# Where the projection slices are computed, and the order of the table rounds, in a two-part kernel on Trainium2

## The chip, the cores and the metric

The kernel runs on one core of one Trainium2 chip. The metric is the device time of one execution in microseconds. A core has five engines with queues of their own, each in order: PE (matrix products), DVE (VectorE), ACT (ScalarE), POOL (GpSimd) and SP (SyncE, which here only starts transfers). They wait for each other by semaphores.

## The reference

Two independent computations share the input and are joined along the last axis:

- Part A, a recurrent memory attention. The sequence of 2048 rows is cut into 64 segments of 32. Each segment attends over 8 memory rows and its own 32, with 32 heads of 128; the first 8 rows of its output are the memory of the next segment. So the segments are sequential.
- Part B, a state space convolution. `K = einsum(C, exp(dt*A*l), dt*B).real` for 2048 positions and 1024 channels, then `irfft(rfft(u)*rfft(K))`, plus `u*Dskip`.

```python
h = jnp.concatenate([mem, xs], axis=1)
q, k, v = (jnp.einsum('btd,dhe->bhte', h, W) for W in (Wq, Wk, Wv))
...
K = jnp.einsum('dn,dnl,dn->dl', Cc, P, dB).real
y = irfft2(rfft2(u) * rfft2(K))[..., :L] + u * Dskip
```

## The kernel before

The order of work is written out by hand: each engine executes its instructions in the order in which the program issues them. In time there are four stretches:

1. **The parameter stage** (0 to about 91 us). DVE and ACT compute, from A, B, C and dt, the log modulus and the angle of each coefficient in float32 (`modulus`, `angle`); `put3` splits each in three bfloat16 parts and stores them to the DRAM tensors PB (cast to `hi` and `mid` on ACT, differences on DVE, stores on SP). Beside that, the generator `matrices` makes the Fourier matrices MF with sines on ACT, two columns a step. The generator `ahead.transposes` (lines 84 to 104) loads x in 16 blocks on POOL's queue, transposes them on PE, and copies each on ACT into `xst`, stored to XTd, and into `xTl`, the 8 last rows of each segment. `run` takes one step of each of its generators in turn.
2. **The table rounds** (91 to about 460 us), the loop `for f in range(-1, 17)`. 16 rounds go over the blocks of 64 channels. Each round takes the words of ORDER one by one. A word is an operation and a slot; with a prime it belongs to the round before. X..t and X..p are the matmuls of the phases (`ptt`, two PSUM buffers) and of the powers (`pa`, one buffer); E is exp, k the shift by a magic constant (both ACT), n the turns (DVE), S the sine (ACT), b the absolute value (DVE), C the cosine (ACT), w the negation `wn` (DVE), gi and gr the products with the exps (DVE, `products`, two instructions each of bfloat16 operands), K the matmuls of kernel values and x their copy to `KxT`. Exp and sine need different tables, so ACT loads a table twice a round. The projections of part A (generator `pro`), the Fourier transform of u (`bg`) and the transposes of MF (`mb`) go along as side work: P, U and M issue their matmuls into a PSUM tile of the pool of four, and p, A, u and m evict it. ON_ACT and ON_DVE say which engine evicts which slot.
   - One slice of `pro` is 8 matmuls of 512 columns (k and q, line 158) or 16 of 256 (v, line 145), and one cast out of PSUM. Two slices use one 512 KB load of weights (`wsl`, four buffers, SP's queue). There are 96 slices; k and q of them need the whole of `xTl`.
   - `bg` (function `side`) yields four pieces per block of u: a copy (r=0), adds on DVE (r=2), a copy (r=1), adds on DVE (r=3). After the last, POOL adds and subtracts the float32 results (`ux`, lines 882 to 885) and stores them to Ud from its own queue. Behind that in POOL's queue stand the four loads of the next round's parameters (`load_par`, issued in E0). The first round already runs U2 and U3, so the pieces fall to the slots in the order 2, 3, 0, 1.
3. **Spectra and inverse transform** (460 to about 720 us). It starts in round 16, at the first word of ORDER, with `negate` on DVE and `spectrum(0)` on PE, beside the rest of the last table.
4. **The 64 segments of part A** (to the end), which read what the projections stored (PKd, XTd).

Four slices of `pro` are issued between the parameter stage and the loop, evicted in turn by ACT and DVE (lines 1110 to 1115); the rounds take six each. The transposes are spread over the two calls of `run` at the end of the parameter stage.

Of the kernel before, what the change touches and what calls it, by code (L numbers as in the profile page):

```python
# [16 lines left out]
PSUM = bass.MemoryType.PSUM  # L17
# [568 lines left out]
def bcast_front(ap, n):  # L586
# [10 lines left out]
NF = NP + NN  # L597
NE, NT = NC + NF, NC + NA
PLEN = 4096
ORDER = ("X0p' X0t' P3' b0' w0' C0' b1' P4' p3' C1' gi0' U2' P5' gr0' k0 n0 P0 E0 gr1' p4' X1t X1p p5' k1 X2t P1 E1 n1 p0 A1' k2 w1' X2p n2 "  # L600
         "X3t E2 U3' gi1' p1 X3p k3 X4t P2 E3 n3 k4 u1' X4p X5t p2 E4 U0 n4 k5 X5p n5 K0' E5 A0 X6p X6t E6 M' X7t k6 m' X7p U1 E7 x0' k7 K1' "
         "u0 K2' x1' S0 n6 K3' x2' n7 S1 x3'").split()
ON_ACT = (('p1', 'P', 1), ('p4', 'P', 4), ('A0', 'U', 0), ('A1', 'U', 2))
ON_DVE = (('p0', 'P', 0), ('p2', 'P', 2), ('p3', 'P', 3), ('p5', 'P', 5), ('u0', 'U', 1), ('u1', 'U', 3), ('m', 'M', 0))


def part_b(ctx, tc, u, A_re, A_im, B_re, B_im, C_re, C_im, log_dt, Dskip, out_b, ahead, copies, residents, first_state):
# [6 lines left out]
    v, sc, gp, pe, sy = nc.vector, nc.scalar, nc.gpsimd, nc.tensor, nc.sync  # L614
# [8 lines left out]
    ident = const.tile([128, 128], BF16, name="b_ident")  # L623
# [9 lines left out]
    tabs = ctx1.enter_context(tc.tile_pool(name="b_tab", bufs=1))  # L633
# [5 lines left out]


    with tc.tile_pool(name="b_par", bufs=1) as par, tc.tile_pool(name="b_parh", bufs=2) as parh, tc.tile_pool(name="b_mg", bufs=2) as mg, \
            tc.tile_pool(name="a_prx", bufs=4) as prx, tc.tile_pool(name="a_ppt", bufs=4, space=PSUM) as ppt:
        ldt = par.tile([128, 8], BF16, name="ldt")
        sy.dma_start(out=ldt[:], in_=log_dt.rearrange("(t p) -> p t", p=128))
        nat = {}
# [7 lines left out]
        def f32(name):  # L653
            return par.tile(sh, F32, name=name)

        def put3(x, q, row):
            hi = parh.tile(sh, BF16, name="hi", tag="hi")
            sc.copy(out=hi[:], in_=x[:])
            sy.dma_start(out=PB[q][row].rearrange("t p n -> p t n"), in_=hi[:])
            yield  # L660
            v.tensor_tensor(out=x[:], in0=x[:], in1=hi[:], op=ALU.subtract)
            mid = parh.tile(sh, BF16, name="mid", tag="mid")
            sc.copy(out=mid[:], in_=x[:])
            sy.dma_start(out=PB[q][row + 1].rearrange("t p n -> p t n"), in_=mid[:])
            yield
            lo = parh.tile(sh, BF16, name="lo", tag="lo")
            v.tensor_tensor(out=lo[:], in0=x[:], in1=mid[:], op=ALU.subtract)
            sy.dma_start(out=PB[q][row + 2].rearrange("t p n -> p t n"), in_=lo[:])
            yield

        def run(*gens):
            gens = list(gens)
            while gens:
                for g in list(gens):
                    if next(g, g) is g:
                        gens.remove(g)
# [11 lines left out]
        def some(g, n):  # L688
            for _ in range(n):
                next(g, None)  # L690
                yield
# [7 lines left out]
        def matrices():  # L699

            tms, kMs = {}, {}
            for c in range(0, 20, 2):
                if 4 <= c:
                    tm = tms.pop(c - 4)
                    v.tensor_scalar(out=tm[:].bitcast(I32), in0=tm[:].bitcast(I32), scalar1=0x7FFFFFFF, scalar2=None, op0=ALU.bitwise_and)
                    sc.activation(out=sines(c - 4, 0), in_=columns(tm), func=ACT.Sin, scale=-TWO_PI, bias=hp[:])
                if 2 <= c < 18:
                    tm = tms[c - 2]
                    v.scalar_tensor_tensor(out=tm[:], in0=kMs.pop(c - 2)[:], scalar=MAGIC, in1=tm[:], op0=ALU.subtract, op1=ALU.subtract)
                    sc.activation(out=sines(c - 2, 1), in_=columns(tm), func=ACT.Sin, scale=-TWO_PI)  # L710
                if c < 16:
                    tms[c] = mg.tile([128, 2, 512], F32, name="tm", tag="tm", bufs=4)
                    for i in range(2):
                        v.tensor_scalar(out=tms[c][:, i], in0=colk[:], scalar1=rowl[:, c + i:c + i + 1], scalar2=None, op0=ALU.mult)
                    kMs[c] = mg.tile([128, 2, 512], F32, name="mkM", tag="mkM")
                    sc.activation(out=kMs[c][:], in_=tms[c][:], func=ACT.Identity, bias=magic[:])
                yield

        dt_b = dtb[:].unsqueeze(2).to_broadcast(sh)
        mats = matrices()  # L720
# [23 lines left out]
        v.tensor_scalar(out=low[:], in0=pF[:, 2:3], scalar1=-1.0, scalar2=1.0, op0=ALU.mult, op1=ALU.add)  # L744
        tI = par.tile([128, 8], I32, name="tI")
        gp.iota(tI[:], pattern=[[1, 8]], base=0, channel_multiplier=0)
        own = par.tile([128, 8], F32, name="own")
        v.tensor_copy(out=own[:], in_=tI[:])
        v.tensor_scalar(out=pF[:, 3:4], in0=pF[:, 0:1], scalar1=47.5, scalar2=None, op0=ALU.is_lt)
# [6 lines left out]
        for ts in par_t:  # L756
            for t_ in ts:
                gp.memset(t_[:], 0.0)
        x1, x2, x3, x4, x5, Wr, Wi = (f32(n_) for n_ in ("x1", "x2", "x3", "x4", "x5", "Wr", "Wi"))

        y1, y2 = f32("y1"), f32("y2")
# [12 lines left out]
        def modulus():  # L774

            sc.activation(out=y1[:], in_=Wi[:], func=ACT.Square)
            sc.activation(out=y2[:], in_=Wr[:], func=ACT.Square)
            yield
            v.tensor_tensor(out=x4[:], in0=y1[:], in1=y2[:], op=ALU.add)
            v.tensor_scalar(out=x4[:], in0=x4[:], scalar1=1.0e-37, scalar2=None, op0=ALU.max)  # L780
            sc.activation(out=x4[:], in_=x4[:], func=ACT.Ln)

            sc.activation(out=y1[:], in_=Wr[:], func=ACT.Abs)
            sc.activation(out=y2[:], in_=Wi[:], func=ACT.Abs)
            yield
            v.tensor_scalar(out=x4[:], in0=x4[:], scalar1=0.5, scalar2=None, op0=ALU.mult)
            yield

        def angle():

            v.tensor_tensor(out=x5[:], in0=y1[:], in1=y2[:], op=ALU.max)
            v.tensor_scalar(out=x5[:], in0=x5[:], scalar1=1.0e-37, scalar2=None, op0=ALU.max)
            v.reciprocal(out=x5[:], in_=x5[:])
            v.tensor_tensor(out=x3[:], in0=y1[:], in1=y2[:], op=ALU.min)
            v.tensor_tensor(out=x3[:], in0=x3[:], in1=x5[:], op=ALU.mult)
            sc.activation(out=x3[:], in_=x3[:], func=ACT.Arctan)
            yield
            v.tensor_scalar(out=x3[:], in0=x3[:], scalar1=float(1.0 / TWO_PI), scalar2=None, op0=ALU.mult)
            v.tensor_tensor(out=y1[:], in0=y2[:], in1=y1[:], op=ALU.is_gt)
            v.tensor_scalar(out=y2[:], in0=Wr[:], scalar1=0.0, scalar2=None, op0=ALU.is_lt)  # L800
            v.tensor_scalar(out=Wi[:], in0=Wi[:], scalar1=0.0, scalar2=None, op0=ALU.is_lt)
            yield
            for msk, top in ((y1, 0.25), (y2, 0.5)):
                v.tensor_scalar(out=x5[:], in0=x3[:], scalar1=-2.0, scalar2=top, op0=ALU.mult, op1=ALU.add)
                v.tensor_tensor(out=x5[:], in0=x5[:], in1=msk[:], op=ALU.mult)
                v.tensor_tensor(out=x3[:], in0=x3[:], in1=x5[:], op=ALU.add)
                yield
            v.tensor_scalar(out=Wi[:], in0=Wi[:], scalar1=-2.0, scalar2=1.0, op0=ALU.mult, op1=ALU.add)
            v.tensor_tensor(out=x3[:], in0=x3[:], in1=Wi[:], op=ALU.mult)
            yield  # L810
            yield from put3(x3, 1, 3)

        xs = ahead.transposes(prx, ppt, ident)
        pro = ahead.projections()
        next(pro)
        run(modulus(), put3(x2, 1, 0), put3(x1, 0, 0), some(xs, 9), some(mats, 3))
        run(xs, angle(), xs, put3(x4, 0, 3), xs, mats)


    tmp = ctx1.enter_context(tc.tile_pool(name="b_tmp", bufs=2))  # L820
# [15 lines left out]

    def take(shape, dtype, name):
        return ps_k.tile(shape, dtype, name=name, tag="s")

    def matrices_back():  # L840
        for c in range(16):
# [264 lines left out]
    evict_of = {}  # L1106
    for eng, names in ((sc.copy, ON_ACT), (v.tensor_copy, ON_DVE)):
        for nm, kind, slot in names:
            evict_of[nm] = (kind, slot, eng)
    evict = pro.send((take, tabs))  # L1110
    for i in range(3):
        evict_next = next(pro)
        evict((sc.copy, v.tensor_copy)[i % 2])
        evict = evict_next
    evict(v.tensor_copy)
    for f in range(-1, 17):
        if f == 15:
            for kind, slot in sorted(k for k in pending if k[0] == "P"):
# [4 lines left out]
        if f == 16:  # L1123
            spectra = [load_u(0), load_u(1)]
        for word in ORDER:
            nm, r = word.rstrip("'"), f - word.endswith("'")
            if f == 16 and word == ORDER[0]:
                s0 = ps_e.tile([128, 2, 512], F32, name="pa", tag="pa")
# [315 lines left out]
```

## Time and profile before

| | |
|---|---|
| median of 12 runs | 2388.78 us (2375.84 to 2398.88) |
| the profiled execution | 2382.18 us, its span 2380.5 us |
| busy in the span | PE 1997.1, DVE 1469.0, ACT 976.3, POOL 361.8 us |
| first exp of the first round | 94.15 us |
| first sine of the first and of the last round | 114.44 and 459.19 us |
| last KxT copy of the last round | 476.20 us |

The spans are those of one execution taken by the hardware profiler. In lines of the timeline the first two numbers are start and duration in us, and brackets tell how long the engine idled before and what ended it. DVE and ACT overlap the end of an instruction with the start of the next, so that a duration is some 0.08 to 0.13 us longer than the distance from start to start.

### The profile page before, as it was taken

Reading aid. Unit: us, or ns where it says so; the run is one execution under the profiler, and the core shown is the slowest. Engines: PE = TensorE matmul, PEld = TensorE weight load, DVE = VectorE, ACT = ScalarE, POOL = GpSimd, SP = SyncE. Lnnn points to the kernel's source line nnn. Section 1 sums busy time; section 2 is a strip of 40 time slices with the busy share of each in tenths; the row PEclk is TensorE's granted clock in tenths of the full one; section 3 lists DMA queues with packets and bytes.
Section 4 is the critical chain, followed back from the end, with each engine's and each line's share of the span. In section 5 each row is a group of like instructions: output and inputs, shape, how many; then the busy total and the mean of one; then the engine's idle time right before and its main releaser. Section 6 shows DMA issues by size and latency. Waiting matters only on the chain.

```text
span 2380.5 us, 78431 instructions
## 1 busy us (share of the span) xinstructions
PE 1997.1 (84%) x33798; PEld 1177.8 (49%) x33798; DVE 1469.0 (62%) x3160; ACT 976.3 (41%) x1599; POOL 361.8 (15%) x623
## 2 busy tenths in 40 slices
PE   1699999779997888888888888888888888888879
PEld 1366665668883444444444444444444444444444
DVE  9599999999963545455454555545445455554540
ACT  6699999713242333232333323333233232322320
POOL 2245354572220000000000000000000000000020
PEclk6799999889997999999999999999999999999999
DMA  6786885684489999999999999999999999999991
GB/s 160 187 241 198 248 228 150 185 267 154 149 288 366 391 383 384 385 383 384 360 377 385 370 379 387 380 381 376 392 352 378 380 377 382 384 364 378 383 395 62
DMA packets 379680, 759.08 MB, mean 319 GB/s; under 512 B 121704, under 2 KB 213000, under 8 KB 377284
## 3 DMA queue, kind: packets, MB, share of 16 engines
q1 hardware_dynamic: 364116, 709.89, 82.9%
q0 software_dynamic: 15216, 44.18, 5.6%
q8 instruction: 264, 4.33, 0.7%
q14 instruction: 84, 0.69, 0.1%
HBM read 699.16 MB, written 67.88 MB: 322 GB/s over the span
## 4 chain that ended last, share of the span: by engine, by line
DMA 33%; PE 30%; DVE 19%; issue 9%; ACT 6%; POOL 2%; SPq 1%; DVEq 0%; ACTq 0%; POOLq 0%
DMA wst<-WD_k 16%; PE acc L349 11%; DMA wst<-WD_o 9%; PE pp L448 4%; PE pe L571 2%; PE pro L158 2%; DVE nr L1068 2%; DMA wst<-WD_v 2%; DMA out_dram<-uu 2%; PE ups L866 2%; PE tr L360 2%; DMA wst<-WD_q 2%; PE pa L1037 2%; DVE piece L282 1%; DMA KT<-Kd 1%
## 5 line engine op out<-in xcount | busy, mean ns | idle before, releaser
L349 PEld LDWEIGHTS <-hT 128*32 128x32 bf16 x12352 | 325.8, 96 | 465.1 <-issue 239.8
L349 PE MATMUL acc<-wst,hT 128*32 128x512 bf16 x3072 | 312.1, 390 | 157.9 <-DMA wst<-WD_k 61.1
L349 PE MATMUL acc<-W,hT 128*32 128x512 bf16 x5120 | 400.8, 384 | 0.0
L355 ACT CAST ev<-acc 128x512 bf16<-128x512 f32 x384 | 224.7, 585 | 397.3 <-PE acc L349 391.9
L448 PEld LDWEIGHTS <-oT 128*32 128x32 bf16 x8192 | 203.6, 97 | 111.6 <-issue 85.3
L282 DVE TENSOR_SCALAR piece<-keep 128x256 int32<-128x256 int32 (+1 forms) x640 | 190.9, 361 | 53.8 <-PE pp L448 33.3
L387 DVE TENSOR_REDUCE mx<-sc 128x8 f32<-128x320 f32 x128 | 62.2, 486 | 246.0 <-PE sc L380 246.0
L448 PE MATMUL pp<-W_o,oT 128*32 128x256 bf16 x4096 | 183.1, 276 | 5.3 <-DMA W_o<-in_A_Wo_dram 5.2
L361 DVE COPY KT<-tr 128x512 bf16<-128x512 bf16 x64 | 27.2, 424 | 257.7 <-PE tr L360 257.7
L349 PE MATMUL acc<-MF,hT 128*32 128x512 bf16 x2048 | 158.2, 383 | 0.0
L368 POOL COPY KT<-pk 128x128 bf16<-128x128 bf16 x128 | 37.7, 294 | 793.3 <-PE sc L380 449.6
L448 PE MATMUL pp<-wst,oT 128*32 128x256 bf16 x2560 | 128.7, 278 | 34.4 <-DMA wst<-WD_o 25.2
L361 ACT COPY QT<-tr 128x512 bf16<-128x512 bf16 x128 | 74.9, 586 | 192.7 <-PE tr L360 191.8
L435 ACT CAST oT<-pv 128x512 bf16<-128x512 f32 x128 | 75.0, 586 | 168.1 <-PE pv L421 166.0
L321 POOL COPY hT<-xt 128x192 bf16<-128x192 bf16 x63 | 21.9, 347 | 727.6 <-DMA xt<-XTd 506.0
L158 PE MATMUL pro<-xTl,wsl 128*128 128x512 bf16 x512 | 118.7, 382 | 5.8 <-ACT xTl L102 5.2
L1007 PEld LDWEIGHTS <-MF 128*128 128x128 bf16 x1024 | 102.8, 101 | 29.2 <-issue 10.1
L389 ACT ACTIVATE sc<-sc 128x320 f32<-128x320 f32 x128 | 54.0, 422 | 153.7 <-DVE sc L388 146.9
L360 PEld LDWEIGHTS <-ev 128*128 128x128 bf16 x1024 | 58.1, 98 | 97.0 <-issue 67.7
L1007 PE MATMUL hps<-KT,MF 128*128 128x256 bf16 x720 | 94.9, 284 | 13.3 <-DVE x L1182 10.2
L1239 PE MATMUL yp<-Bt,MI 128*128 128x256 bf16 x680 | 102.8, 273 | 0.8 <-ACT yb L1255 0.8
L360 PE MATMUL tr<-a_ident,ev 128*128 128x128 bf16 x1024 | 102.2, 223 | 0.0
(315 smaller groups left out, 3791.8 us busy)
## 6 DMA issues: line engine op xcount, KB each, us to landing
wst<-WD_o SPq DMA_DIRECT2D x320, 512.0 KB
wst<-WD_k SPq DMA_DIRECT2D x256, 512.0 KB
wst<-WD_q SPq DMA_DIRECT2D x256, 512.0 KB
wst<-WD_v SPq DMA_DIRECT2D x256, 512.0 KB
Ud<-ux POOLq DMA_DIRECT2D x16, 1024.0 KB, 5.6
uq<-Ud SPq DMA_DIRECT2D x32, 512.0 KB
pk<-PKd SPq DMA_DIRECT2D x64, 192.0 KB
wsl<-in_A_Wk_dram SPq DMA_DIRECT2D x16, 512.0 KB
```

Source lines behind the costliest of these rows:

```text
L158: nc.tensor.matmul(a[:], lhsT=w[:, kc, 128 * j:128 * j + 128], rhs=xTl[:, kc, :, :].rearrange("p s k -> p (s k)"), start=(kc == 0), stop=( ...
L282: nc.vector.tensor_scalar(out=out.bitcast(I32), in0=in_.bitcast(I32), scalar1=0, scalar2=None, op0=ALU.bitwise_or)
L349: nc.tensor.matmul(a[32 * g:32 * g + 32, o_:o_ + rhs.shape[1]], lhsT=hT[:, kc, :], rhs=rhs, start=(kc == 0), stop=(kc == KC - 1), tile_pos ...
L355: nc.scalar.copy(out=q[:], in_=a[:])
L360: nc.tensor.transpose(out=p[:, i, hl, :, :].rearrange("p a b -> p (a b)"), in_=q[:, 128 * hl:128 * hl + 128], identity=ident[:])
L361: eng(out=dst, in_=p[:, i, :, :, :])
L387: nc.vector.tensor_reduce(out=mx[:], in_=sc, axis=AX.X, op=ALU.max)
L389: nc.scalar.activation(out=sc, in_=sc, func=ACT.Exp, scale=scale)
L435: nc.scalar.copy(out=o[:], in_=p[:].rearrange("p a (g q) -> p a g q", g=4))
L448: nc.tensor.matmul(po[32 * qt:32 * qt + 32, :], lhsT=oT[:, h % 4, (h % 16) // 4, :], rhs=columns(w, 1024 * hh + 256 * qt, 256)[0][1], star ...
L1007: pe.matmul(s_[r][half][:, cs, :], lhsT=MF[:, kc, 4 * rr + mc, cs, :], rhs=rhs, start=(i == 0 and mc == 0), stop=(i == 1 and mc == 3), ski ...
L1239: pe.matmul(yp[:, b, :], lhsT=m_[:, b, cs, kc, :], rhs=Bt[:, kc, j, half, c_, :], start=(kc == 0 and cs == 0 and half == 0), stop=(kc == 3 ...
```

## The change

Sixteen slices of the projections are now issued in the parameter stage, and the rounds take five each.

- The transposes begin earlier: the first loads of x go out ahead of the parameters' first products, six blocks are transposed and copied before `modulus`, and the rest between the steps of `modulus` and the first `put3`.
- Behind them the slices are issued step by step beside `angle`, `put3(x4)` and the rest of `matrices`, into three PSUM tiles of a pool of their own, and all 16 are evicted by ACT, two slices late.
- `run` gives `matrices` two steps beside `modulus`, three beside `angle`, and the rest afterwards (before: three, then the rest beside `angle`).
- ORDER is new: five P a round (slots 0 to 4), another rotation (a round now begins with gi0' instead of X0p'), and other places for most words. u0 stands behind gi0' and gr0' of the next round; b0, w0, C0, b1 and C1 stand at the end of their own round.
- ACT evicts slices 1 and 3, DVE 0, 2 and 4 (before: ACT 1 and 4, DVE 0, 2, 3 and 5).

```diff
-ORDER = ("X0p' X0t' P3' b0' w0' C0' b1' P4' p3' C1' gi0' U2' P5' gr0' k0 n0 P0 E0 gr1' p4' X1t X1p p5' k1 X2t P1 E1 n1 p0 A1' k2 w1' X2p n2 "
-         "X3t E2 U3' gi1' p1 X3p k3 X4t P2 E3 n3 k4 u1' X4p X5t p2 E4 U0 n4 k5 X5p n5 K0' E5 A0 X6p X6t E6 M' X7t k6 m' X7p U1 E7 x0' k7 K1' "
-         "u0 K2' x1' S0 n6 K3' x2' n7 S1 x3'").split()
-ON_ACT = (('p1', 'P', 1), ('p4', 'P', 4), ('A0', 'U', 0), ('A1', 'U', 2))
-ON_DVE = (('p0', 'P', 0), ('p2', 'P', 2), ('p3', 'P', 3), ('p5', 'P', 5), ('u0', 'U', 1), ('u1', 'U', 3), ('m', 'M', 0))
+ORDER = ("gi0' X0p' P2' gr0' X0t' X1t u0' P3' E0 gr1' p1' X1p U2' E1 p2' k0 X2p U3' E2 n0 w1' k1 X3p gi1' X2t E3 P4' k2 p3' n1 A1' n2 X4p "
+         "X3t E4 M u1' X4t k3 X5p U0 E5 n3 k4 X6p X5t E6 n4 K0' p4' k5 X7p A0 m X6t K1' E7 n5 k6 x0' X7t x1' P0 n6 k7 S0 n7 K2' p0 K3' x2' "
+         "S1 b0 U1 x3' w0 C0 P1 b1 C1").split()
+ON_ACT = (('p1', 'P', 1), ('p3', 'P', 3), ('A0', 'U', 0), ('A1', 'U', 2))
+ON_DVE = (('p0', 'P', 0), ('p2', 'P', 2), ('p4', 'P', 4), ('u0', 'U', 1), ('u1', 'U', 3), ('m', 'M', 0))
...
+            tc.tile_pool(name="a_pps", bufs=3, space=PSUM) as pps:
...
+        xs = ahead.transposes(prx, ppt, ident)
+        pro = ahead.projections()
+        next(pro)
+        next(xs)
...
+        for _ in range(2 * 6):
+            next(xs)
...
-        run(modulus(), put3(x2, 1, 0), put3(x1, 0, 0), some(xs, 9), some(mats, 3))
-        run(xs, angle(), xs, put3(x4, 0, 3), xs, mats)
+        run(modulus(), xs, xs, put3(x2, 1, 0), xs, put3(x1, 0, 0), xs, some(mats, 2), xs)
+        takes = [lambda shape, dtype, name: pps.tile(shape, dtype, name=name, tag="s")]
+        evicts = [pro.send((lambda *a: takes[0](*a), tabs))]
+
+        def projected(n):
+            for _ in range(n):
+                evicts.append(next(pro))
+                if len(evicts) > 2:
+                    evicts.pop(0)(sc.copy)
+                yield
+        first_slices = projected(16 - 1)
+        run(angle(), first_slices, put3(x4, 0, 3), some(first_slices, 4), some(mats, 3))
+        run(mats, first_slices)
+        while evicts:
+            evicts.pop(0)(sc.copy)
...
-    evict = pro.send((take, tabs))
-    for i in range(3):
-        evict_next = next(pro)
-        evict((sc.copy, v.tensor_copy)[i % 2])
-        evict = evict_next
-    evict(v.tensor_copy)
```

More of the change, by code (lines that the diff above doesn't have):

```diff
@@ L641, in part_b @@
     with tc.tile_pool(name="b_par", bufs=1) as par, tc.tile_pool(name="b_parh", bufs=2) as parh, tc.tile_pool(name="b_mg", bufs=2) as mg, \
-            tc.tile_pool(name="a_prx", bufs=4) as prx, tc.tile_pool(name="a_ppt", bufs=4, space=PSUM) as ppt:
+            tc.tile_pool(name="a_prx", bufs=4) as prx, tc.tile_pool(name="a_ppt", bufs=4, space=PSUM) as ppt, \
+            tc.tile_pool(name="a_pps", bufs=3, space=PSUM) as pps:
         ldt = par.tile([128, 8], BF16, name="ldt")
@@ L811, in angle @@
             yield from put3(x3, 1, 3)
-        xs = ahead.transposes(prx, ppt, ident)
-        pro = ahead.projections()
-        next(pro)
-        run(modulus(), put3(x2, 1, 0), put3(x1, 0, 0), some(xs, 9), some(mats, 3))
-        run(xs, angle(), xs, put3(x4, 0, 3), xs, mats)
+        run(modulus(), xs, xs, put3(x2, 1, 0), xs, put3(x1, 0, 0), xs, some(mats, 2), xs)
[12 more added lines that the diff above has]
+            evicts.pop(0)(sc.copy)
     tmp = ctx1.enter_context(tc.tile_pool(name="b_tmp", bufs=2))
@@ L838, in take @@
         return ps_k.tile(shape, dtype, name=name, tag="s")
+    takes[0] = take
     def matrices_back():
```

## The prediction

> **What bounds the kernel now.** I read the busy table in stages first, to find the part that the change touches, then the timeline of each engine over one table round, then the groups of the few instructions whose duration varies.
>
> Busy time by stage (columns: window, length, PE, weight loads, DVE, ACT, POOL, granted clock, DMA share, GB/s):
>
> ```profile
> 20.00:40.00 20.00, 0.49 (x6) 0.49 (x6) 17.95 (x22) 18.21 (x19) 0.00 (x0) 0.53 0.44 99
> 60.00:80.00 20.00, 6.03 (x48) 5.09 (x48) 15.76 (x19) 17.60 (x24) 2.58 (x5) 0.50 0.62 145
> 200.00:220.00 20.00, 18.24 (x225) 11.03 (x224) 18.63 (x29) 19.06 (x22) 10.51 (x12) 1.00 0.52 160
> ```
>
> The parameter stage (to about 91 us) is ACT and DVE handing work to each other while PE idles at half clock. The rounds (91 to 460 us) have PE, DVE and ACT all above 90% busy: three engines share the bound, and any wait that one of them gains lengthens the round. ACT's timeline gives the first and last round's sines:
>
> ```profile
> 114.44 1.75 ACT L1062 ACTIVATE sn<-nr 128x1856 bf16<-128x1856 f32 x1
> ...
> 459.19 3.39 ACT L1062 ACTIVATE sn<-nr 128x1856 bf16<-128x1856 f32 x2
> ```
>
> So 15 rounds take 344.75 us, 22.98 each. Now DVE and POOL of one round, from the timeline (start, duration):
>
> ```profile
> 204.90 0.69 DVE L877 TENSOR_TENSOR us<-ua,ups 128x512 f32<-128x512 f32 x1 [0.54 <-PE ups L866]
> ...
> 208.27 1.58 DVE L1068 TENSOR_SCALAR nr<-nr 128x1856 int32<-128x1856 int32 x1
> 209.77 0.88 DVE L1075 TENSOR_SCALAR wn<-sn 128x768 bf16<-128x768 bf16 x1
> 210.57 1.66 DVE L1068 TENSOR_SCALAR nr<-nr 128x1856 int32<-128x1856 int32 x1
> ...
> 212.75 1.11 DVE L1019 TENSOR_TENSOR gi<-E,sn 128x1824 bf16<-128x1824 bf16 x1
> ...
> 219.78 0.35 DVE L1075 TENSOR_SCALAR wn<-sn 128x768 bf16<-128x768 bf16 x1
> ```
>
> ```profile
> 205.68 1.26 POOL L882 TENSOR_TENSOR ux<-us 128x512 f32<-128x512 f32 x1 [0.78 <-DVE us L877]
> 206.91 1.27 POOL L883 TENSOR_TENSOR ux<-us 128x512 f32<-128x512 f32 x1
> 208.14 4.67 POOL L885 TENSOR_TENSOR ux<-us 128x256 f32<-128x256 f32 x4
> ```
>
> The same negation wn takes 0.35 us when POOL is silent and 0.88 beside the sums. Lining up the two: a small sum ends at 208.86, abs runs to 209.85, the next sum runs, then wn, then a sum, then abs. They take turns, each waiting for the other's whole instruction. This costs DVE about 0.45+0.53+0.53=1.5 us a round, and ACT idles 0.53 before its second cosine. The products gi and gr come just as the sums end; all 64 first pieces last 1.10 to 1.12. In this trace no product ever meets a sum.
>
> **The change, part by part.**
>
> *Twelve slices move into the parameter stage.* A slice is 8 matmuls at 0.216 = 1.73 us of PE and one cast (0.48 start to start on ACT). ACT idles 9.2 us before 18.4 and 6.0 before 51.4, where the transposes' copies (0.97 a block) now fit, so xTl is whole at about 50 instead of 83, and PE has room. I followed the order of ACT and DVE with the rows' start-to-start times: the six early blocks make the squares 4 us later, but ACT catches up under DVE's reciprocal (6.55), arctan comes at 50.7 (51.4 before), and since two steps of the matrices now come behind the angle (0.69+1.22+0.88 of DVE each), the last third of x3 is done at 76.6 (81.4 before). On ACT follow six sines and shifts, two casts and a table load; first exp at 87.4, before 94.15. On SP six wsl loads (4th to 9th) now stand between the stores of the parts; the last waits for the tenth slice on PE, due at about that time: nothing, and up to 3 us if PE stays at half clock (its first 8 matmuls took 0.427 each). The eight u_h loads are issued 6 us earlier and still hold back the third exp by some 3 us. Sum at the first sine of the first round: 105.6 against 114.4, **−9 us** (bounds −13, and 0 if every saving is lost to waits between ACT, PE and SP).
>
> *Five slices a round.* PE loses 1.73 us, DVE one cast of 0.60; ACT keeps two casts. On ACT, which alone fills 21.15 of 22.98, nothing is taken away but waits.
>
> *The new order.* What starts POOL's sums is the eviction u0 (two DVE adds, 0.60 each): the side generator begins with U2 and U3 in the first round, so slot 1 is the fourth quarter. In the order before, u0 stood ahead of the sine, and abs, wn, abs met the sums. Now u0' stands behind gi0' and gr0', and the next on DVE are gr1' (two instructions), a cast, n0, w1', gi1' (two). So abs is freed (1.5 us saved, ACT's 0.53 idle gone), and four product instructions and wn are put beside the sums. On POOL, the spectrum store and four parameter loads stay behind the sums, with over 6 us to spare.
>
> What a product pays there is not in the trace; bounds: nothing, as every product shows now, or a whole instruction each time, as abs does. I take turns, because the trace shows POOL's side of the same exclusion with a two-input add of DVE: the copy hT<-xt, 0.347 in 63 other places, starts with such an add and ends after it:
>
> ```profile
> 653.67 1.22 DVE L1186 TENSOR_TENSOR y<-uq,x 128x1024 f32<-128x1024 f32 x1
> 653.81 1.27 POOL L1402 COPY hT<-xt 128x192 bf16<-128x192 bf16 x1
> ```
>
> [...] No run so far shows a product held up.
>
> The walk, from the end of the first sine, t=0. abs 1.12 (estimate: 0.69 for 1024 elements; 0.99 in the line-up above), KxT 0.34, wn 0.28, abs 1.12, gi0' 1.52, gr0' 1.52, u0' 1.20: t=7.2. Sums: 1.24, 1.24, then four of 0.62. The first sum began at 6.8, so gr1' waits 0.85, its second piece 1.25 for the second sum; cast and n0 read PSUM and pass freely; wn waits 0.1, the pieces of gi1' 0.6 each: t=15.15, of which **3.4 us waits**. Then n1, n2 1.1, u1' 1.2, n3, n4 1.1, cast 0.60, ms 0.65, n5 0.55: t=20.35. The rest is a chain over engines: phase matmul, shift 0.65, table load 1.28, sine 1.74, 4.2 with handovers. Round 24.6; followed on ACT, 24.9; I take **24.7**, +1.7 a round, 15 rounds **+26**.
>
> Without waits at the products DVE is done with gi1' at 11.7 and ACT sets the round: four sines and two table loads 9.5, eight exps and eight shifts, four evictions 11.6, and 1.35 waiting for power matmuls that queue on PE behind slices and quarters (1.2 now): **22.4**, 15 rounds −8.
>
> *The end of the rounds.* Now from the end of the last first sine (460.9) to the last KxT copy (476.6) it takes 15.7 us. In the new order negate (1.74) comes behind abs instead of ahead, but u0' and its sums lie inside the last products: 20.0 with waits, 16.1 without: **+4** or 0. PE's P1 in round 15 now ends just before negate overwrites xTl; nothing, at most its 1.75. All behind it, from 480 us, is untouched.
>
> Sum: −9+26+4 = **+21 us** on the profiled execution of 2382.2 us (span 2380.5). That execution lies 6.6 under the median of 12, so on the median: 2388.8+21, about **2410**.
>
> **The rivals.**
> 1. *Products pass the sums freely; faster.* For it: the products' constant 1.10 to 1.12, the absence of any example, and that only POOL's side is seen waiting for such an add. Against: taking turns with abs is strict. −9−8+0: −17, 2372. It decides from waits of about 1.2 us a round downward (break-even round 23.4), against the 3.4 of the walk.
> 2. *Waits, but no gain in the parameter stage.* ACT and DVE were 16 to 18 of 20 us busy there, and 14 casts more go to ACT; if PE, casts and wsl loads wait on each other, −9 becomes 0: +30, 2419.
> 3. *Half the waits*: POOL's turn is given up when a product is ready, and only the long sums cost. Round 23.4 to 23.7: −9+9+2, 2391.
>
> **How the numbers follow.** Chances: forecast 0.56, rival 1 0.26, rival 2 0.08, rival 3 0.10. No change means within 0.3% (7 us), about what a measurement of this kernel can tell. Slower 0.56+0.08+0.03, faster 0.26+0.02, same 0.05. Forecast alone: 2400 to 2418. The range must reach rival 1, whose own bounds (parameter gain −13 to −5) are 2368 to 2376, and rival 2: 2369 to 2421.
>
> **What would show it.** Right: the first exp at 87 us; products gr and gi of half 1 at up to 2.3 us in the trace, abs at 1.0 to 1.25; sine to sine 24.7; DVE without idle time but before abs; ACT waiting for nr and kM's matmuls. Wrong: all products still 1.1 and the round at 22.4 (rival 1), or the first exp at 94 or later (rival 2). I would also be wrong if the rounds were set by something that this walk has free, such as PSUM tiles waiting for a late eviction.

## The result, and the profile after

The changed kernel takes 2401.75 us (median of 12 runs, 2396.16 to 2412.55), the kernel before 2387.97 (49 runs). The ratio is 1.0065, with a 95% interval of 1.0049 to 1.0082: slower by 15.5 us, 12 to 20. The profiled execution of the changed kernel is the slowest of its 12 (2412.55 us, span 2410.8), so stages are compared here, not spans.

Busy time of the changed kernel in the three windows that the prediction showed (columns: window, length, PE, weight loads, DVE, ACT, POOL, granted clock, DMA share, GB/s):

```profile
20.00:40.00 20.00, 5.08 (x40) 4.27 (x41) 15.34 (x18) 15.80 (x21) 2.88 (x6) 1.00 0.82 227
60.00:80.00 20.00, 16.91 (x78) 7.47 (x77) 17.61 (x22) 14.33 (x19) 1.17 (x2) 1.00 0.62 154
200.00:220.00 20.00, 17.23 (x244) 13.00 (x242) 18.30 (x28) 18.81 (x22) 7.01 (x9) 1.00 0.60 175
```

PE now works in the parameter stage (16.91 of 20 us where it had 6.03). Its granted clock there is 1.00 (before: 0.53 and 0.50). In the window of the rounds PE is less busy than before (17.23, was 18.24), as it should be with a slice less. ACT's timeline gives the first exponential and the first sine of the first round, and the first sine of the last:

```profile
93.96 0.71 ACT L1064 ACTIVATE E<-pa 128x648 bf16<-128x648 f32 x1
...
110.61 1.75 ACT L1081 ACTIVATE sn<-nr 128x1856 bf16<-128x1856 f32 x1
...
470.86 3.39 ACT L1081 ACTIVATE sn<-nr 128x1856 bf16<-128x1856 f32 x2
```

| | before | after | difference | predicted |
|---|---|---|---|---|
| first sine of the first round | 114.44 | 110.61 | -3.8 | -9 |
| 15 rounds | 344.75 (22.98 each) | 360.25 (24.02 each) | +15.5 | +26 |
| from the end of the last first sine to the last KxT copy | 15.7 | 18.6 | +2.9 | +4 |
| sum | | | +14.6 | +21 |

The sum agrees with the measured 15.5 (the two medians lie 13.8 apart, inside the interval). The first exponential comes at 93.96, no earlier than before (94.15): all but 0.2 of the 3.8 us lie between it and the sine, in the first round's own work, and not in the parameter stage. Each round is 24.10 us; the last, without the next round's table work, 22.83. Behind the last copy, in code that the change does not touch, the profiled executions of all the kernels here need between 1902 and 1923 us, without an order that follows from the kernels; that is why the spans say little.

One round of the changed kernel, DVE's line (start, duration, in brackets idle time before and what ended it):

```profile
215.10 0.68 DVE L897 TENSOR_TENSOR us<-ua,ups 128x512 f32<-128x512 f32 x1
215.70 1.82 DVE L1038 TENSOR_TENSOR gr<-E,nr 128x1824 bf16<-128x1824 bf16 x1
217.44 1.64 DVE L1039 TENSOR_TENSOR gr<-E,nr 128x768 bf16<-128x768 bf16 x1
...
220.14 0.42 DVE L1094 TENSOR_SCALAR wn<-sn 128x768 bf16<-128x768 bf16 x1
220.48 1.64 DVE L1038 TENSOR_TENSOR gi<-E,sn 128x1824 bf16<-128x1824 bf16 x1
222.04 1.09 DVE L1039 TENSOR_TENSOR gi<-E,wn 128x768 bf16<-128x768 bf16 x1
```

and POOL's sums in the same stretch:

```profile
215.28 1.25 POOL L901 TENSOR_TENSOR ux<-us 128x512 f32<-128x512 f32 x1 [10.34 <-DVE us L896]
216.50 2.14 POOL L902 TENSOR_TENSOR ux<-us 128x512 f32<-128x512 f32 x1
218.61 4.10 POOL L904 TENSOR_TENSOR ux<-us 128x256 f32<-128x256 f32 x4
```

The first add of the eviction u0' releases the sums, and the next product, gr1', takes 1.82 instead of 1.11, its second piece 1.64 instead of 0.57, the pieces of gi1' 1.64 and 1.09 instead of 1.12 and 0.57. POOL pays too: its second sum lasts 2.14 instead of 1.27. So the products do take turns with the sums. ACT's line shows one way in which this reaches the round: the fifth exponential waits for the pieces of gi1'.

```profile
223.23 0.71 ACT L1064 ACTIVATE E<-pa 128x648 bf16<-128x648 f32 x1 [0.96 <-DVE gi L1039]
```

The groups of the products over the 15 rounds (count | total us, mean ns | idle before):

```profile
L1038 DVE TENSOR_TENSOR gr<-E,nr 128x1824 bf16<-128x1824 bf16 x30 | 43.2, 1440 | 0.0
L1038 DVE TENSOR_TENSOR gi<-E,sn 128x1824 bf16<-128x1824 bf16 x30 | 40.9, 1363 | 0.0
...
L1039 DVE TENSOR_TENSOR gr<-E,nr 128x768 bf16<-128x768 bf16 x30 | 32.0, 1066 | 0.0
L1039 DVE TENSOR_TENSOR gi<-E,wn 128x768 bf16<-128x768 bf16 x30 | 24.4, 812 | 0.0
```

Where no product meets a sum, the means are 1114, 1118, 568 and 568 (the changed kernel with shifted quarters, below). The differences, times 30, are 39.4 us; with 0.9 for wn it is 2.7 a round. That looked like the whole answer. It is not: the experiments show what 2.7 us of waits are worth, and a second mechanism of which the prediction knew nothing.

### The profile page after: what moved, and what is told of

Its sections match the earlier page's. It is cut to its first block, busy times and chain, and to the rows that moved or that the text cites. A ratio compares the mean times of both kernels' runs of the same rounds, so it can differ in the third digit from the quotient of the medians.

```text
span 2410.8 us, 78433 instructions
## 1 busy us (share of the span) xinstructions
PE 2015.3 (84%) x33798; PEld 1184.2 (49%) x33798; DVE 1481.5 (61%) x3146; ACT 984.6 (41%) x1613; POOL 362.0 (15%) x623
## 4 chain that ended last, share of the span: by engine, by line
DMA 35%; PE 25%; DVE 19%; ACT 10%; issue 8%; POOL 1%; SPq 1%; DVEq 0%; ACTq 0%; POOLq 0%
DMA wst<-WD_k 15%; PE acc L349 12%; DMA wst<-WD_o 10%; PE pp L448 3%; DMA wst<-WD_v 3%; PE pe L571 2%; DMA out_dram<-uu 2%; PE tr L360 2%; DMA wst<-WD_q 2%; ACT kM L1070 2%; ACT E L1064 2%; DVE gr L1038 2%; DVE piece L282 1%; DVE nr L1087 1%; DMA KT<-Kd 1%
```

## The experiments

Ratios are to the kernel before on the same chip, with 95% intervals; rounds and windows are those of one profiled execution of each kernel; "a round" is the mean of 15, from the first sine of the first round to that of the last.

### The sums left out, in both kernels

```diff
-                            x_ = up.tile([128, 4, 2, DQ], F32, name="ux", tag="ux")
-                            gp.tensor_tensor(out=x_[:, 0], in0=e_[:, 0], in1=o_[:, 0], op=ALU.add)
...
-                            gp.dma_start(out=Ud[kc, dq], in_=x_[:])
+                            gp.dma_start(out=Ud[kc, dq][:, 0:2], in_=e_[:])
+                            gp.dma_start(out=Ud[kc, dq][:, 2:4], in_=o_[:])
```

> The changed kernel without GpSimd's twelve sums a round (six instructions): the two halves of the quarter are stored as they are, in two stores, and the spectra that are made of them are then others. Theory (the products of half 1 wait for the sums, 2.9 us a round, and this is what the new order costs): all products 1.10 to 1.12 and 0.56, a round falls from 24.0 to what ACT sets, about 22.4 by the walk of the prediction; 15 rounds -24, the end of the rounds -2.5: about 2375 where the changed kernel has 2402, ratio to the kernel before 0.994. Rival (the products wait, but the round is set by something else in the new order, such as the exponentials that must wait for the products of the table that they overwrite): products 1.10, the round stays at 23.6 to 24.0, ratio 1.003 to 1.006.

> The kernel before, without GpSimd's sums in the same way. Theory: abs falls from 1.6 to 1.1 and wn from 0.88 to 0.35, which frees 1.5 us of DVE and the 0.53 that ACT idles before its second cosine: the round falls from 22.98 to 21.5 to 22.45, ratio 0.990 to 0.997. Rival (abs and wn stand off the path that sets the round): the same durations, but the round stays within 0.1 of 22.98, ratio 0.999 to 1.001.

Measured: the changed kernel without sums 0.9976 (0.9953 to 0.9999), 23.12 a round; the kernel before without sums 0.9945 (0.9922 to 0.9969), 22.07 a round. In both, products are 1.12 and 0.57, abs 1.12, wn 0.35. For the kernel before that is the theory's value. For the changed one it is neither theory nor rival. A window per round shows why: its rounds are of two kinds. Two neighbours (columns as above):

```profile
207.22:230.90 23.68, 21.27 (x282) 16.69 (x277) 19.81 (x33) 21.31 (x26) 3.90 (x7) 0.93 0.75 194
230.90:253.07 22.17, 19.78 (x268) 14.34 (x264) 19.66 (x33) 21.27 (x26) 3.89 (x7) 1.00 0.86 248
```

Where the granted clock is 1.00 the round is 22.17 us; where it is 0.93, 23.68, with the same instructions on DVE and ACT. Eight of the 15 rounds lie between 23.56 and 23.77 at 0.93, a ninth, the last, at 24.28; six are 22.17 to 22.19. ACT's lines of the first of these two rounds show the way:

```profile
219.21 0.71 ACT L1060 ACTIVATE E<-pa 128x648 bf16<-128x648 f32 x1 [0.55 <-PE pa L1052]
...
221.38 0.71 ACT L1060 ACTIVATE E<-pa 128x648 bf16<-128x648 f32 x1 [0.92 <-PE pa L1052]
```

Two exponentials wait for their matmuls, 1.47 us together; in the other round no exponential waits for PE. So two questions come apart. With full clock the sums cost the new order 24.10-22.17=1.93 a round and the old one 22.98-22.07=0.91. And the clock costs 1.5 us in a round that loses it.

### The old order with five slices, then with TensorE kept busy

The first kernel has the changed parameter stage and the old ORDER without P5' and p5'. The second multiplies the slice of slot 0 twice into the same PSUM tile, which gives PE back the 1.73 us that the sixth slice took, and changes nothing else:

```diff
-                    for b in (2 * j, 2 * j + 1):
+                    for b in (2 * j, 2 * j + 1) * (2 if self.twice else 1):
...
-                    for kc in range(KC):
+                    for kc in list(range(KC)) * (2 if self.twice else 1):
...
     def run_side(kind, slot):
+        ahead.twice = kind == "P" and slot == 0
```

> The change without its new order: sixteen slices in the parameter stage, and the rounds in the order before with one of its six slices left out. Theory (the part of the change that pays is the moved slices, the part that costs is the order): first sine 3.8 earlier as in the changed kernel, the round shorter by up to one cast (0.60) of DVE, 22.4 to 22.98; ratio 0.995 to 0.998. Rival (moving slices is what made the time longer): ratio 1.003 or more.

> The old order with five slices and sixteen in the parameter stage, with the slice of the first slot multiplied twice, in the place where the sixth slice stood: TensorE works what it worked before the change. Theory (the 24.8 us a round of that kernel come from TensorE's pause of 2.9 us and the half clock behind it): granted clock 1.00, round 22.4 to 23.0, ratio 0.995 to 1.000. Rival (it is the shifted use of PSUM tiles or of the queues): the round stays above 24, ratio 1.010 or more.

Measured: 1.0133 (1.0105 to 1.0161) with 24.76 a round, the slowest kernel of all, though it only leaves work out of the rounds: so the rival holds, moving slices does make the time longer, for a reason that it did not name. Its first sine was expected 3.8 us earlier than before the change and came 2.4 later, at 116.84; so the moved slices alone gain nothing there, and the 3.8 of the changed kernel need its new order too. With the useless slice added, 1.0004 (0.9985 to 1.0023) with 22.84 a round. Here is PE in a round of the first kernel, with the wait for the first exponential in brackets:

```profile
222.77 0.36 PE L1050 MATMUL ptt<-RT,pt 128*128 128x464 bf16 x1
226.05 0.70 PE L1056 MATMUL pa<-RE,pt 128*128 128x324 bf16 x2 [2.92 <-ACT E L1064]
226.54 0.59 PE L1050 MATMUL ptt<-RT,pt 128*128 128x464 bf16 x1
226.93 2.89 PE L145 MATMUL pro<-wsl,xTl 128*128 128x256 bf16 x16
```

and its windows of one us from 224 to 230:

```profile
224.00:225.00 1.00, 0.00 (x0) 0.00 (x0) 1.00 (x2) 1.00 (x1) 1.00 (x3) 1.00 1.12 427
225.00:226.00 1.00, 0.00 (x0) 0.00 (x0) 0.90 (x3) 0.99 (x3) 0.25 (x1) 0.75 1.03 388
226.00:227.00 1.00, 0.95 (x4) 0.47 (x4) 1.00 (x2) 1.00 (x3) 0.00 (x0) 0.50 0.96 277
227.00:228.00 1.00, 1.00 (x7) 0.67 (x6) 1.00 (x3) 1.00 (x4) 0.00 (x0) 0.50 1.02 258
...
229.00:230.00 1.00, 1.00 (x11) 0.85 (x9) 1.00 (x2) 0.00 (x0) 0.00 (x0) 1.00 0.80 198
```

PE must wait for the first exponential, which frees the only tile `pa`. Before the change the sixth slice filled that gap down to 1.17 to 1.27 us in the rounds between the first and the last (0.47 in one), and the doubled slice does so too (1.18 to 1.27); a round of the kernel before, and one of the kernel with the doubled slice:

```profile
216.72 0.44 PE L1037 MATMUL pa<-RE,pt 128*128 128x324 bf16 x2 [1.27 <-ACT E L1045]
```

```profile
243.34 0.44 PE L1057 MATMUL pa<-RE,pt 128*128 128x324 bf16 x2 [1.22 <-ACT E L1065]
```

Without it the gap is 2.92 us, the granted clock falls to 0.50 for some 3 us, and the next slice takes 2.89 instead of 1.91; the matmuls of the exponentials stand behind it on PE, and ACT idles (0.00 in the last window; its waits for `pa` are 33.6 us between 130 and 440, in the kernel before 12.0). All 15 rounds are at a clock of 0.87 or 0.93. With the slice multiplied twice the clock is 1.00 in all 15, and the waits for `pa` are 9.5. So the sixth slice was free where it stood, and taking it out cost about 1.9 us a round in the old order. It is PE's pause that did it, not the use of tiles or queues, as these stay as they are in the second kernel. How much of it is the wait itself and how much the clock behind it is not told apart here, since no round of the first kernel kept its clock.

### u0 behind gi1

```diff
-ORDER = ("gi0' X0p' P2' gr0' X0t' X1t u0' P3' E0 gr1' p1' X1p U2' E1 p2' k0 X2p U3' E2 n0 w1' k1 X3p gi1' X2t E3 P4' k2 ...
+ORDER = ("gi0' X0p' P2' gr0' X0t' X1t P3' E0 gr1' p1' X1p E1 p2' P4' k0 X2p E2 n0 w1' k1 X3p gi1' u0' U2' X2t E3 U3' k2 ...
```

U2' and U3' move behind it, P4' and its eviction come earlier, so that PSUM tiles come free in order, and in the part that is not shown U1 and P1 change places.

> The changed kernel with the eviction u0 (whose two adds release GpSimd's sums) moved from behind gr0 to behind gi1, the second quarter and third and fourth slices moved so that PSUM tiles come free in order. The sums then stand beside turns, casts and evictions, which read PSUM. Theory: no product, abs or wn waits, the round is 22.4, the end of the rounds 2 shorter, ratio to the kernel before 0.993 to 0.996. Rival (the quarter that is started 4 us later holds back TensorE, and through it the power matmuls and exponentials): products 1.10, but the round at 23 to 24 with ACT waiting for pa, ratio 0.998 to 1.006.

Measured: 1.0061 (1.0035 to 1.0087), 23.94 a round. The products are back at 1.12 and 0.57, and yet the round with full clock is 23.68. The rival's round of 23 to 24 us holds. Waits between 130 and 440 us (total, times, longest):

```profile
DVE nr L1076 <- ACT kM L1070: 31.7, 36, 2.0
...
ACT E L1064 <- PE pa L1056: 16.8, 25, 2.1
```

In the changed kernel the same lines have 4.6 and 10.7. A round with full clock shows what stands in the way:

```profile
220.70 1.91 PE L145 MATMUL pro<-wsl,xTl 128*128 128x256 bf16 x16
...
222.92 0.71 ACT L1064 ACTIVATE E<-pa 128x648 bf16<-128x648 f32 x1 [0.97 <-PE pa L1056]
```

The slice of slot 4 now runs on PE between the matmuls of the second and of the third exponential, and ACT waits 0.97 for it; with two more waits (0.36 and 0.16) that is 1.49 us, the distance from 22.17 to 23.68. So what costs most is a slice that was moved along with the quarter, and less the late quarter that the rival named. DVE, which no longer waits at the products, waits for ACT. A removed wait is a gain only if the order leaves the next engine ready.

### The quarters shifted

The sums can be moved without moving anything in the order: the four pieces of a block are counted from another slot, so that u1 instead of u0 ends a block. DVE is then at turns, casts and evictions, which read one operand from SBUF at most and one from PSUM.

```diff
-                if f >= 0:
+                if f >= 0 and not (f == 0 and word in ("U2'", "U3'")):
                     run_side(nm[0], int(nm[1:] or 0))
```

> The kernel before with the four quarters of a block shifted by two of the round's slots, so that the eviction u1 instead of u0 ends a block and releases GpSimd's six sum instructions. They then stand beside turns, casts and evictions, which read PSUM, and end before abs. Theory (a DVE instruction that reads SBUF alone pays beside the sums, one that reads PSUM doesn't): abs 1.1, wn 0.35, the round 22.07 as in the kernel without sums, 15 rounds -14, ratio 0.994. Rival (the sums cost the same wherever they stand, only other instructions pay): the round 22.7 to 23.0, ratio 0.998 to 1.000.

> The changed kernel with the same shift; nothing is left out. Theory: no product waits; the rounds are those of the changed kernel without sums, 22.17 where TensorE keeps its clock and 23.67 where the 2 us in which it waits for the first exponential cost it its clock (0.93 in the mean of a round); by how many there are of each, mean 22.2 to 23.7, ratio 0.993 to 1.002. Rival (the order itself costs more than its waits): 24 us a round, ratio 1.005.

> The same, and one slice of the round (the third slot, ahead of the matmuls that wait for the first exponential) is multiplied twice into the same PSUM tile: 1.73 us of TensorE more a round, nothing else. Theory (TensorE's pause of 2 us costs it its clock, and the slower matmuls then hold up ACT): granted clock 1.00 in every round, all rounds 22.1 to 22.3, although TensorE has more to do; ratio 0.991 to 0.995. Rival (the clock falls for another reason, or the slower matmuls hold up nobody): rounds as in the run before it or longer by what the slice takes, ratio no lower than there.

Measured: the kernel before with the shift 0.9944 (0.9921 to 0.9966), 22.08 a round. Its groups of abs and wn (count | total us, mean ns | idle before):

```profile
L1068 DVE TENSOR_SCALAR nr<-nr 128x1856 int32<-128x1856 int32 x30 | 34.6, 1153 | 4.0 <-ACT sn L1062 4.0
L1075 DVE TENSOR_SCALAR wn<-sn 128x768 bf16<-128x768 bf16 x30 | 10.4, 348 | 0.0
```

abs was 1614 and wn 614 in the mean. The sums lose their stretching as well (1.27, 1.27 and 0.72 a piece), and what stands beside them keeps its time: turns 0.63 us, casts 0.68, the adds of the evictions 0.68 each (0.63, 0.68 and 0.68 in the means of the kernel before). So here the instructions that read PSUM did not wait for the sums, where abs and wn, which read SBUF alone, had waited 0.46 and 0.27 in the mean. The theory holds; what lies behind it is not shown.

The changed kernel with the shift: 0.9979 (0.9961 to 0.9996), 22.73 a round. Four rounds at the start and the last are at a clock of 0.93, ten at 1.00:

```profile
183.56:207.31 23.75, 20.96 (x240) 12.70 (x238) 19.87 (x33) 21.31 (x26) 9.59 (x13) 0.93 0.64 202
207.31:229.56 22.25, 19.79 (x282) 15.88 (x278) 19.70 (x33) 21.29 (x26) 8.18 (x12) 1.00 0.90 218
```

With the slice of slot 3 multiplied twice as well, every round is at 1.00 and all but the last are 22.16 to 22.22:

```profile
205.32:227.54 22.22, 21.54 (x299) 17.51 (x294) 19.65 (x33) 21.28 (x27) 9.18 (x13) 1.00 0.84 211
227.54:249.71 22.17, 21.42 (x282) 15.90 (x280) 19.67 (x33) 21.27 (x26) 9.15 (x13) 1.00 0.81 245
```

PE does 1.7 us more a round and the round is shorter by 0.5 in the mean. The whole kernel comes to 0.9964 (0.9943 to 0.9985), above the 0.991 to 0.995 of the theory and not told apart from the 0.9979 without the doubled slice, so the gain is shown in the rounds alone: the doubled slice also stands in the first round, ahead of the second exponential, and the first sine came at 116.6 instead of 112.5, which gives back 4.2 of the 7.7 us.

In the changed kernel as it is, six rounds have a clock of 0.93 too, and all but the last are 24.09 to 24.11, with the clock or without:

```profile
182.90:207.00 24.10, 20.08 (x243) 11.90 (x239) 22.40 (x33) 21.51 (x26) 10.80 (x12) 1.00 0.68 216
399.82:423.92 24.10, 21.23 (x243) 12.75 (x239) 22.40 (x33) 21.42 (x26) 10.80 (x12) 0.93 0.43 133
```

There the slow matmuls hide behind DVE, which stands at the products: in the second of these rounds two exponentials wait 0.91 and 0.56 us for PE, in the first none of them does, but the fifth waits 0.96 for the products, and from the next shift on both rounds are at the same point. So the clock does not explain the 24.10; it would have taken a part of what a better place for the sums gives.

### Why the first sine came 3.8 us earlier and not 9

Two waits were not in the prediction's walk. On ACT, the copies of the transposes wait for the stores of the copies before (four buffers), and the squares come at 26.2, before the change at 18.4:

```profile
23.39 0.80 ACT L101 COPY xst<-pt_x 128x768 bf16<-128x768 bf16 x1 [7.42 <-DMA XTd<-xst]
```

On PE, the round's first slice waits for the last two casts of the parameter stage, which stand behind the matrices' last six instructions on ACT:

```profile
92.70 3.46 PE L145 MATMUL pro<-wsl,xTl 128*128 128x256 bf16 x16 [5.19 <-ACT kst L167]
```

One kernel moves the casts, another gives the copies eight buffers:

```diff
-        run(mats, first_slices)
         while evicts:
+            run(some(mats, 1))
             evicts.pop(0)(sc.copy)
+        run(mats)
```

```diff
-            xst = pool.tile([128, 4, self.KC, self.XM], BF16, name="xst", tag="xst")
+            xst = pool.tile([128, 4, self.KC, self.XM], BF16, name="xst", tag="xst", bufs=8)
```

> The changed kernel with the last casts of the parameter stage's sixteen slices put between the last steps of the matrices instead of behind them. Theory (the prediction's 9 us of gain shrank because TensorE's next slices wait 5.2 us for the PSUM tiles that these casts free): that wait is 0 to 1.5 us, the second exponential comes at 94 to 95.5 instead of 98.6, the first sine at 106 to 108, the rest as in the changed kernel: 3 to 4 us off its 2402, ratio 1.003 to 1.006. Rival (the u_h loads hold back the third exponential anyway): first sine at 110 to 111.

> The changed kernel with eight buffers instead of four for the transposes' copies. Theory (the squares come 7.8 us late since ACT stands behind the stores of these copies, and that is what is missing of the prediction's gain): squares at 18 to 20, arctan at 48 to 51 instead of 55.2, first exponential at 88 to 90, first sine at 105 to 107. Rival (ACT and TensorE wait elsewhere behind that: for weights, for casts): squares early, but the first exponential within 1.5 us of 94.

Measured with early casts: 1.0064 (1.0043 to 1.0086). The wait is 2.91, the second exponential comes at 95.55, but PE then waits for u_h (1.13 at 98.11), and the first sine is at 108.98, 1.6 earlier: between theory and rival, and too little for the comparison to show.

```profile
98.11 1.03 PE L886 MATMUL ups<-u_h,MF 128*128 128x256 bf16 x8 [1.13 <-DMA u_h<-in_B_u_dram]
```

Measured with eight buffers: 1.0029 (1.0010 to 1.0048). Squares at 19.9, arctan at 50.49 (the walk had 50.7), first exponential at 90.74, first sine at 107.28, 3.3 us earlier:

```profile
90.74 0.71 ACT L1064 ACTIVATE E<-pa 128x648 bf16<-128x648 f32 x1
95.29 0.71 ACT L1064 ACTIVATE E<-pa 128x648 bf16<-128x648 f32 x1 [3.84 <-PE pa L1056]
```

That is just outside the theory's ranges, and far from the rival. The stores account for most of the missing 5 us, the late casts for a part.

### Everything together

The changed kernel with the shift, the doubled slice of slot 3 from the second round on, eight buffers, early casts, and the u_h loads issued ahead of the rounds; beside it the kernel before with the shift alone.

> The changed kernel with the shifted quarters, the doubled third slice (from the second round on), the early casts, the eight copies and the first u_h loads issued ahead of the first round's slices. If the effects add: first sine 104 to 107, 22.2 a round, the end of the rounds as in the shifted kernel; 2388 -9 -12 = 2364 to 2369, ratio 0.990 to 0.992. If what is won in the parameter stage is lost to loads that now come together: first sine 110 to 113, ratio 0.993 to 0.995.

> The kernel before with the shifted quarters once more, beside the one with everything, on the same chip: ratio 0.992 to 0.997 as measured. If the sums are all that is to be won, the kernel with everything is no faster than this; if moving slices early has a worth of its own, it is 4 to 9 us faster.

Measured: 0.9915 (0.9896 to 0.9935), a median of 2369.4 us; the shift alone 0.9940 (0.9920 to 0.9960), 2377.0 us. ACT's sines of the first and last round in the kernel with everything:

```profile
104.95 1.75 ACT L1084 ACTIVATE sn<-nr 128x1856 bf16<-128x1856 f32 x1
...
438.14 3.39 ACT L1084 ACTIVATE sn<-nr 128x1856 bf16<-128x1856 f32 x2
```

The first sine comes 9.5 us earlier than in the kernel before, the rounds (22.21 each) give 11.6 and their end 1.2, 22.2 together; the ratio says 20.3, 15.5 to 25. Both kernels beat the two that the change is about. Beside the shift alone, the kernel with everything is 7.5 us lower in the median of six executions each; its first sine is 8.3 us earlier (104.95 against 113.22), while its 15 rounds are 2.3 longer. So moving slices early seems to have a worth of its own once its waits are gone, but the intervals of the two kernels overlap a little, and the early u_h loads without the moved slices were not tried, so how much is open.

## Why the prediction was right, and where not

The sign and the range hold, and the forecast (2410) is 8 us above the median. Part of that nearness is luck: the first sine missed its forecast by +5.2 us and the rounds theirs by -10.5, and the two errors half cancel.

*Products take turns with the sums: right.* The walk had 3.4 us of waits a round, the groups say 2.7; gr1' waits 0.7 and 1.1 where 0.85 and 1.25 stood. The row that led to it, a POOL copy stretched by a two-input add of DVE (1.27 us, 0.35 in its 63 other places), showed the right side of the same exclusion.

*The length of a round: the mechanism right, the size off.* The forecast took 24.7, the trace shows 24.10, and 24.02 with the shorter last round, so 15.5 instead of 26 us. Of the 0.6 between 24.7 and 24.10, 0.2 lies in the round without waits (22.4 in the walk, 22.17 in the runs at full clock) and 0.4 in what the waits add (2.3 us for 3.4 in the walk, 1.93 for 2.7 in the runs). So the share of a wait that reaches the round was about right, and the waits themselves were taken 0.7 too long. The rest of the 10.5 is the last round, which the forecast took as long as the others.

*abs is freed of 1.5 us: right in kind.* abs fell from 1.61 to 1.12 and wn from 0.61 to 0.38. What the old waits had cost the round is 0.91 (the kernel before without sums, and again with the shift). So the change moved the sums from a place where they cost 0.91 to one where they cost 1.93; the rest of the new order costs 0.10 at full clock (22.17 against 22.07).

*PE loses a slice: the step that was missing.* It was listed as a loss of work without effect on the pace. It has one: the slice filled a gap, and without it PE paused for 1.9 to 3.0 us and in some of the rounds fell to a clock of 0.50 for about 3. In the changed kernel this is hidden behind the waits, so that the forecast did not suffer from it; in the old order it costs 1.9 us a round.

*The parameter stage, -9: wrong in size and in place.* The walk had the first exponential at 87.4, 6.8 us earlier, and some 2 more up to the sine. The first exponential came at 93.96, 0.2 earlier, and the way from there to the sine took 16.65 us instead of 20.29. The stores behind the copies and the casts behind the matrices held it up: the walk followed ACT and DVE and gave four buffers and a tile of PSUM no time. The bounds of -13 and 0 held the -3.8.

*The end of the rounds, +4:* +2.9.

Rival 2, no gain in the parameter stage, was half right: its sign, a first exponential at 94 or later, was missed by 0.04 us, and only the first round's work kept its sum from coming true. Rival 1 (2372) fell since the products do wait; its 22.4 for a round without waits was close to the 22.17 of the runs. Rival 3's round of 23.4 to 23.7 was nearer to the 24.02 than the forecast's 24.7, but its mechanism is not what the trace shows: POOL does not give up its turn, and the short sums cost too (the pieces of gi1').

## What to carry to other kernels

When work is taken off an engine that waits in between, look at what the gap becomes: TensorE with 1.7 us less to do made the rounds of the old order 1.9 us longer (24.76 against 22.84). Before an order is written anew to part two instructions that contend, see whether the contending work can be released from another place: counting the pieces from another slot was one line and took 0.6% off the kernel before. And one engine's waits hide another's; take each away alone, with the clock read round by round, before adding the gains.

## What the runs showed of the hardware

TensorE's granted clock fell to 0.50 behind pauses as short as 2 us, and not behind all of them (in the changed kernel 0.50 from 410 to 413 us, behind a pause of 2.01). In three kernels (the changed one, the one without sums and the one with the shift) PE waits 1.9 to 2.0 us for the first exponential in 13 of the rounds (one of the changed kernel's shows 1.25): 15 of these 39 rounds lose their clock. In the two kernels with the same rounds as the changed one (early casts, eight buffers) 10 of 26 do. Of 13 rounds with 2.1 to 2.4 us (u0 behind gi1) two do, of 13 with 2.9 to 3.0 (old order, five slices) all, but the last one of u0 behind gi1, with 2.93, does not; and of the rounds with at most 1.6 us (the kernel before up to its last round, the doubled slice in the old order) none. So the length alone does not decide, and in these kernels 2 us were often too many. What sets which rounds lose the clock was not tried.

DVE's products and POOL's sums alternated instruction by instruction in the changed kernel: in the round shown the second sum took 2.14 us instead of 1.27, the pieces of gr1' 1.82 and 1.64 instead of 1.11 and 0.57, each longer by 0.7 to 1.1, about what was left of the other's instruction.
